# A spectral mix and a mixture of experts on one core: input pieces loaded as 112 rows plus one shared row, and four moves in the opening order

## The chip, the cores and the metric

The kernel runs on one core of a Trainium2 chip. The metric is device time in microseconds (us) of one execution. The kernel before takes 635.36 us (median of 3 runs, 635.27 to 635.87). The five engines are named here as the profile names them: PE (TensorE matmuls) with its weight loads PEld, DVE (VectorE), ACT (ScalarE), POOL (GpSimd), and SP, which only issues transfers.

## The reference

The kernel computes, for 2048 tokens `x` of width 448, a gated sum of two branches:

```python
g = sigmoid((x * gate_w).sum(-1, keepdims=True))
# branch a: real part of a 2-D Fourier transform by matrices
a_ = x @ dft_hid_re.T ; b_ = x @ dft_hid_im.T
a  = dft_seq_re @ a_ - dft_seq_im @ b_
# branch b: 8 experts, the two best per token
gates = softmax(x @ wg); top 2, renormalised -> cw
h = gelu(einsum("nd,edf->nef", x, w1)) ; y = einsum("nef,efd->ned", h, w2)
b = einsum("ne,ned->nd", cw, y)
out = g * a + (1 - g) * b
```

## The kernel before

**Stages.** From about 38 us to the end PE runs the experts, one unit (expert, 128 of its 1792 inner columns) after another: the first layer (line 752) and the second (line 803). The change lies wholly in the 38 us ahead of that, the opening, which has three jobs: the routing's logits and, from them, the list of the tokens of the first expert; the hidden-axis Fourier transform; and the sequence-axis transform. Both transforms use the matrices' mirror symmetry, so the tokens come as eight input pieces.

**Input pieces.** Piece (c, r), c = 0 to 3 and r = 0 or 1, is a slab of 128 partitions by 1024 numbers (4 KB per partition). A partition holds one hidden index; only the first 113 (`HH`) hold data, the rest zeros. SP issues the eight loads (line 102) in the order c, r, with the hidden matrix `wr` behind the fourth, then `spec` and the four sequence matrices `cw` (line 107). ACT's own queue issues one load, the logits' weights `wgr` (line 98). Each load signals one of eight semaphores in turn; a load that comes to a semaphore in use waits on SP for the load that had it.

**PE in the opening.** `logits(c)` (line 474) multiplies raw pieces with `wgr`; `flip(c)` (line 481) transposes the result, and after `flip(3)` the routing starts. `hidden(v)`, v = 0 to 7, called block v below, is the hidden transform of one folded half (line 512); ACT copies its result from PSUM to the tile `ab` (line 513). `even(m)`, m = 0 to 3 (line 453), multiplies the matrix `cw` m with blocks 0 to 3, in two halves of two products each; `odd(m, v)` (line 555) multiplies it with block v = 4 to 7, one product each. In the trace an f32 product is two matmul instructions with a weight load each, so an even(m) is 8 and an odd(m, v) is 2 of them, and a block 8. `turn_over(n)` (line 116) issues n matmuls on zeros.

**DVE in the opening.** Each piece is folded in three steps: `fold_near` (line 488), `fold_half` (lines 492 and 493) and `fold_quarter` (line 505). A fold_quarter(c, r) makes what block 2c + r multiplies. Between folds stands the routing, a generator whose steps `advance()` issues. Its steps here: the marks `mb` of each token's two experts (lines 243 to 256, DVE); the running counts `pt` (lines 259 to 262, PE, 18 matmuls); each token's position at the first expert, ending in the tile `ov` (lines 272 to 288, DVE); two short DVE lines for `dz` (291 and 292); the token list (line 296 on PE, line 300 as casts `tok` on DVE and ACT), from which POOL gathers rows (line 532); and on ACT the exponential `ex` with a load of the table for the next function behind it (lines 304 and 305).

**ACT behind it.** ACT then rounds the first two weight tiles (`upper`, line 205, four instructions, `hi` and `up` each) and only then copies blocks 6 and 7.

**What sets the order.** PE, DVE, ACT and SP run in the order in which the code issues; nothing is rescheduled. Each engine takes its instructions in that order, so one that waits holds all behind it.

Of the kernel before, what the change touches and what calls it, by code (L numbers as in the profile page):

```python
# [9 lines left out]
F32 = mybir.dt.float32  # L10
# [5 lines left out]
OP = mybir.AluOpType  # L16
AX = mybir.AxisListType

P = 128
# [28 lines left out]
NQT = QT // P  # L48
# [2 lines left out]
HD = D // 2 + 1  # L51
HE = HD + 1
HH = HE // 2
NL = 32
LOTS = (0, NF)
BANKS = (0, 1, 2, 4, 3)
# [15 lines left out]
def tile_kernel(ctx: ExitStack, tc: tile.TileContext, xt, xrows, xplain, wg, whid, cq, cw, cspec, edge, refs, wquad, whall, cgen, wcat, out):  # L72
    nc = tc.nc
    te, ve, se, gp, sp = nc.tensor, nc.vector, nc.scalar, nc.gpsimd, nc.sync
# [15 lines left out]
    hp = hid_stack.enter_context(tc.tile_pool(name="hid", bufs=2))  # L90
    XR = {}
# [4 lines left out]
    CW = [abp.tile([P, 2, NQT, P], F32, name="cw", bufs=NQT) for _ in range(NQT)]  # L96
    spec = keep.tile([P, 3 + NQT], F32, name="spec")
    se.dma_start(wgr, wg)
    for c in range(NQT):
        XR[c] = hp.tile([P, 2, 2, 2, 2, P], F32, name="xraw", bufs=NQT)  # L100
        for r in range(2):
            sp.dma_start(XR[c][:, r], xt[c + r * NQT])
        if c == 1:
            sp.dma_start(wr, whid)
    sp.dma_start(spec, cspec)
# [351 lines left out]
    def advance(n=1):  # L457
        for _ in range(n):
            next(route, None)
# [6 lines left out]
    def logits(c, *rs):  # L466
        if c not in LT:
            LT[c] = psy.tile([P, P], F32, name=f"y{1 + c % 2}")
        for s in range(4):
            cc, far = divmod(s, 2)  # L470
            for h in range(2):
                for r in rs:
                    j = 32 * (2 * h + r)
                    te.matmul(LT[c][j : j + 32], wgr[:, cc, far], XR[c][:, r, cc, far, 1 - h if far else h], start=s == 0, stop=s == 3, tile_position=(0, j))  # L474

    def evacuate(c):
        LT[c, 1] = hp.tile([P, P], F32, name="lgt")
# [5 lines left out]
    def fold_near(c, *rs):  # L483
        if c not in PQ:
            PQ[c] = hp.tile([P, 2, 2, 2, P], F32, name="pq")
            EO[c] = hp.tile([P, 2, 2, 2, P], F32, name="eo")
        for r in rs:
            ve.tensor_tensor(PQ[c][:, r], XR[c][:, r, :, 0], XR[c][:, r, :, 1], OP.add)

    def fold_half(c, r):  # L490
        raw, pq, eo = XR[c], PQ[c], EO[c]
        ve.tensor_tensor(eo[:, r, 0], pq[:, r, :, 0], pq[:, r, :, 1], OP.add)
        ve.tensor_tensor(eo[:, r, 1], pq[:, r, :, 0], pq[:, r, :, 1], OP.subtract)
        if c == 0:
            if r.start:
                ve.tensor_copy(xs, eo[:, 1, 0, :, 0:1].to_broadcast([P, 2, P]))
                for k in range(2):
                    ve.tensor_tensor(eo[:, k, 0, :, 0:1], raw[:, 0, :, 0, k, 0:1], raw[:, 0, :, 1, 1 - k, 0:1], OP.add)
                ve.memset(eo[:, 0, 1, :, 0:1], 0.0)

    def fold_quarter(c, *rs):
        if c not in FH:
            FH[c] = hp.tile([P, 2, 2, 2, P], F32, name="fr", bufs=NQT)
        for r in rs:
            ve.tensor_tensor(FH[c][:, r], EO[c][:, 0], EO[c][:, 1], OP.subtract if r else OP.add)

    def hidden(v):
        fr = FH[v // 2][:, v % 2]
        acc = ps.tile([P, 512], F32, name="acc")
        for u in range(2):  # L510
            for c in range(2):
                te.matmul(acc[:, 256 * u + HH * c : 256 * u + HH * (c + 1)], fr[:, u, c], wr[:, u, c], start=True, stop=True)  # L512
        se.activation(ab[:, v], halves(acc), AF.Copy)

    def special():
        acc = ps.tile([P, 512], F32, name="acc")
        for c in range(2):
            te.matmul(acc[:, HH * c : HH * (c + 1)], xs[:, c], wr[:, 0, c], start=True, stop=True)
        se.activation(mid[:, 1], acc[:, :HE], AF.Copy)


# [5 lines left out]
    def gather0(c, n):  # L527
        if c < FULL:
            XG[c] = r32(stream.tile([P, DX], F32R, name=("hi", "lo", "up", "dn")[c], bufs=3 if c < 2 else 4))
        else:  # L530
            XG[c] = xp.tile([P, NQ, P], F32, name="xg", bufs=2).rearrange("p q d -> p (q d)")
        gp.indirect_dma_start(out=XG[c][:n], out_offset=None, in_=xplain,
                              in_offset=bass.IndirectOffsetOnAxis(ap=rt["tok0"][:n, c : c + 1], axis=0))
# [8 lines left out]
    def even(m, between=None):  # L542
        acc = ps.tile([P, 512], F32, name="acc")
        for part in range(2):
            run_steps(acc[:, 256 * part : 256 * part + HE], [source(m, part, c) for c in (0, 1)])
            if between and part == 0:
                between()
        se.activation(fold[:, m, :, 0], halves(acc), AF.Copy)
# [44 lines left out]
    flip(3)  # L593
    fold_near(2, slice(0, 2))
    fold_half(2, slice(0, 2))
    fold_quarter(2, 0)
    se.activation(ch[:, :, 0:1], spec[:, 3:, None], AF.Copy)
    special()
    even(0)
    advance()  # L600
    even(1)
    advance()
    fold_quarter(2, 1)
    advance()
    for k in range(3):
        fetch(k)
    even(2)
    even(3)
    hidden(4)
    fold_near(3, 0)  # L610
    advance(2)
    for c, n in enumerate(tl0[:FULL]):
        gather0(c, n)
    hidden(5)
    advance()
    for v in (4, 5):
        for m in range(NQT):
            odd(m, v)
    upper(0)
    upper(1)  # L620
    fold_near(3, 1)
# [661 lines left out]
```

## Time and profile before

| | |
|---|---|
| median of 3 runs | 635.36 us (635.27 to 635.87) |
| profiled execution | 634.15 us |
| its span, first to last instruction | 632.2 us |
| PE busy in the span | 621.9 us (98%) |
| first matmul of the first expert (line 752) | 38.09 us |

A row of the timeline gives start, duration, engine, line, operation, out<-in and a count of merged instructions; in brackets stands the idle time of the engine ahead of it and what ended it. The ends of matmuls are modelled, so a merged row of PE overlaps the next one slightly; for pace the starts of weight loads (PEld) are the better clock.

### The profile page before, as it was taken

To read this page: it belongs to the slowest core of one execution; us is meant where nothing else is said; L and a number is where in the kernel's file an instruction comes from. 1 tells how busy PE (TensorE), PEld (TensorE's weight loads), DVE (VectorE), ACT (ScalarE), POOL (GpSimd) and SP (SyncE) were. 2 spreads that over 40 slices of the span, in tenths; PEclk is the share of its full clock that TensorE was granted. 3 is DMA by queue.
4 is the path that set the end of the run, shared out by engine and by line. 5 is a ranking of instruction groups with operands and counts; after the bars stand their busy time and mean duration, and the time that the engine had idled before them with its cause. 6 is when DMAs were issued, how large, how long until landed. Compare 5 with 4: busy or idle time off the path is not lost.

```text
span 632.2 us, 10955 instructions
## 1 busy us (share of the span) xinstructions
PE 621.9 (98%) x3595; PEld 557.2 (88%) x3595; DVE 503.4 (80%) x1258; ACT 289.4 (46%) x588; POOL 214.3 (34%) x194
## 2 busy tenths in 40 slices
PE   8999999999999999999999999999999999999994
PEld 5999999999998999989999788888888888888884
DVE  7889798679977999779896799988997778655560
ACT  2553233555565566564664434333343334434440
POOL 1210074645144353244450344333241442141123
PEclk9999999999999999999999999999999999999999
DMA  8546454597777777786776867879566737666755
GB/s 332 197 146 218 151 190 147 153 255 235 219 224 191 205 244 227 223 199 196 239 238 211 202 190 244 255 203 281 179 216 192 152 119 156 159 143 143 147 83 64
DMA packets 58751, 122.77 MB, mean 194 GB/s; under 512 B 8288, under 2 KB 31984, under 8 KB 58688
## 3 DMA queue, kind: packets, MB, share of 16 engines
q1 hardware_dynamic: 47376, 101.95, 49.7%
q0 software_dynamic: 11168, 20.00, 18.1%
q8 instruction: 30, 0.49, 0.3%
q14 instruction: 33, 0.27, 0.1%
q10 hardware_dynamic: 144, 0.07, 0.0%
HBM read 105.89 MB, written 16.08 MB: 193 GB/s over the span
## 4 chain that ended last, share of the span: by engine, by line
PE 93%; issue 3%; POOL 1%; DMA 1%; DVE 1%; POOLq 0%; ACT 0%; DVEq 0%; ACTq 0%
PE acc L752 45%; PE y L803 42%; PE y L820 1%; PE acc L512 1%; PE y L555 1%; POOL out L856 1%; PE y L474 1%; DMA wgr<-wg 1%; PE acc L453 0%; POOL out L1019 0%; PE acc L404 0%; PE y L116 0%; PE y L667 0%; PE acc L667 0%; POOLq L1050 0%
## 5 line engine op out<-in xcount | busy, mean ns | idle before, releaser
L752 PE MATMUL acc<-X,hi 128*128 128x288 f32 (+3 forms) x1050 | 215.6, 342 | 0.0
L637 POOL DMA_INDIRECT xg<-xrows,piece x115 | 126.3, 1098 | 210.5 <-DVE xq L646 127.8
L752 PEld LDWEIGHTS acc<-X,hi 128*128 128x128 f32 x1050 | 173.6, 188 | 19.4 <-issue 1.1
L803 PE MATMUL y<-dn,gh 128*128 128x448 f32 (+1 forms) x458 | 167.3, 365 | 0.0
L803 PE MATMUL y<-up,gh 128*128 128x448 f32 (+1 forms) x458 | 167.3, 365 | 0.0
L803 PE MATMUL y<-up,gl 128*128 128x448 f32 (+1 forms) x444 | 162.5, 366 | 0.0
L756 ACT ACTIVATE g<-acc 128x288 f32<-128x288 f32 (+3 forms) x126 | 61.9, 491 | 194.8 <-issue 109.2
L752 PE MATMUL acc<-X,lo 128*128 128x288 f32 (+3 forms) x672 | 134.6, 322 | 0.0
L752 PEld LDWEIGHTS acc<-X,lo 128*128 128x128 f32 x672 | 105.6, 188 | 10.2
L856 POOL DMA_INDIRECT out<-ys,tok x36 | 65.4, 1817 | 115.4 <-ACT ys L852 75.6
L770 DVE TENSOR_TENSOR gl<-g,gh 128x512 fp32r<-128x512 f32 (+1 forms) x111 | 76.5, 689 | 21.1 <-ACT gh L767 15.0
L803 PEld LDWEIGHTS y<-up,gh 128*128 128x128 f32 (+1 forms) x458 | 85.8, 187 | 7.5
L803 PEld LDWEIGHTS y<-dn,gh 128*128 128x128 f32 (+1 forms) x458 | 85.8, 187 | 7.5
L897 DVE CUSTOM_DVE_ANT_0 junk<-quads 128x512 f32<-128x512 f32 x128 | 87.9, 687 | 2.2
L803 PEld LDWEIGHTS y<-up,gl 128*128 128x128 f32 (+1 forms) x444 | 83.2, 187 | 7.1 <-DVE gl L770 0.2
L210 DVE TENSOR_TENSOR lo<-raw,hi 128x512 fp32r<-128x512 f32 x112 | 77.0, 687 | 1.6 <-ACT hi L205 0.6
L769 DVE CAST gh<-g 128x512 fp32r<-128x512 f32 (+2 forms) x69 | 30.2, 438 | 58.6 <-ACT g L756 58.3
L205 ACT ACTIVATE hi<-raw 128x512 fp32r<-128x512 f32 x112 | 69.4, 619 | 0.0
L210 DVE TENSOR_TENSOR dn<-row,up 128x448 fp32r<-128x448 f32 x112 | 69.1, 617 | 0.0
L205 ACT ACTIVATE up<-row 128x448 fp32r<-128x448 f32 x112 | 63.3, 565 | 0.0
L754 ACT ACTIVATE g<-acc 128x256 f32<-128x256 f32 x42 | 16.1, 383 | 49.2 <-PE acc L752 48.8
L1019 POOL DMA_DIRECT2D out<-ot x16 | 13.9, 866 | 60.2 <-ACT ot L1018 60.2
(265 smaller groups left out, 434.9 us busy)
## 6 DMA issues: line engine op xcount, KB each, us to landing
quads<-cq SPq DMA_DIRECT2D x64, 512.0 KB, 5.2
raw<-wcat SPq DMA_DIRECT2D x112, 256.0 KB, 3.0
row<-wcat SPq DMA_DIRECT2D x112, 224.0 KB, 3.5
out<-yt SPq DMA_DIRECT2D x21, 224.0 KB, 3.4
xraw<-xt SPq DMA_DIRECT2D x8, 512.0 KB, 7.0
out<-ot POOLq DMA_DIRECT2D x16, 224.0 KB, 3.9
cw<-cw SPq DMA_DIRECT2D x4, 512.0 KB, 9.5
xg<-xrows,piece POOLq DMA_INDIRECT x115, 3.6
```

Source lines behind the costliest of these rows:

```text
L205: se.activation(hi[:, : raw.shape[-1]], raw, AF.Copy)
L210: ve.tensor_tensor(lo[:, :n], raw, r32(hi[:, :n]), OP.subtract)
L637: st = gp.indirect_dma_start(out=xg[:, q], out_offset=None, in_=xrows, in_offset=bass.IndirectOffsetOnAxis(ap=rt["piece"][:, e, g : g + 1] ...
L752: te.matmul(acc[:, :m], a, b, start=s == 0, stop=s == len(steps) - 1)
L754: se.activation(g[:, cs], acc[:, n : 2 * n], AF.Copy)
L756: se.activation(g[:, cs], g[:, cs] if both else acc[:, :n], AF.Gelu_apprx_tanh)
L769: ve.tensor_copy(gh[:, :top], g[:, :top])
L770: ve.tensor_tensor(gl[:, :main], g[:, :main], r32(gh[:, :main]), OP.subtract)
L803: te.matmul(Y[c][:m, :D], a, b, start=f == 0 and s == 0, stop=f == NF - 1 and s == len(steps) - 1)
L856: st = gp.indirect_dma_start(out=out, out_offset=bass.IndirectOffsetOnAxis(ap=rt["tok"][:n, e, c : c + 1], axis=0), in_=ys[:n], in_offset= ...
L897: ve.tensor_tensor_reduce(out=junk[:, :512], in0=row(a[0])[:, a[1] * 512 : a[1] * 512 + 512], in1=row(b[0])[:, b[1] * 512 : b[1] * 512 + 5 ...
L1019: st = gp.dma_start(out[i * P : (i + 1) * P, :], ot[:, :D], accum_op=OP.add)
```

## The change

The code does four things.

1. The eight input loads carry 112 partitions instead of 128 (`EVEN = 112`), into one tile `xraw`. Partition 112 of all eight pieces comes in one load of 8 rows of 4 KB, issued on ACT's queue behind `wgr`. The folds and products on the pieces read 113 partitions.
2. fold_quarter(2, 0) moves from ahead of the marks to behind them; fold_quarter(2, 1) moves from behind the counts to behind block 4, which puts it behind the positions on DVE; fold_near(3, 0) moves behind the token list.
3. The first half of even(2), two products, moves ahead of the counts.
4. Block 5 moves behind the four odd(m, 4).

```diff
+EVEN = 112
...
     se.dma_start(wgr, wg)
+    xraw = hp.tile([P, 2, NQT, 2, 2, 2, P], F32, name="xraw", bufs=1)
+    se.dma_start(xraw[EVEN:HH].rearrange("p r c a f h t -> p (r c) (a f h t)"), xt[:, EVEN:HH].rearrange("k p a f h t -> p k (a f h t)"))
     for c in range(NQT):
-        XR[c] = hp.tile([P, 2, 2, 2, 2, P], F32, name="xraw", bufs=NQT)
+        XR[c] = xraw[:HH, :, c]
         for r in range(2):
-            sp.dma_start(XR[c][:, r], xt[c + r * NQT])
+            sp.dma_start(xraw[:EVEN, r, c], xt[c + r * NQT, :EVEN])
...
     fold_half(2, slice(0, 2))
-    fold_quarter(2, 0)
     se.activation(ch[:, :, 0:1], spec[:, 3:, None], AF.Copy)
     special()
     even(0)
     advance()
     even(1)
-    advance()
-    fold_quarter(2, 1)
+    fold_quarter(2, 0)
+    even(2, advance)
     advance()
     for k in range(3):
         fetch(k)
-    even(2)
     even(3)
     hidden(4)
+    fold_quarter(2, 1)
+    advance(2)
     fold_near(3, 0)
-    advance(2)
     for c, n in enumerate(tl0[:FULL]):
         gather0(c, n)
+    for m in range(NQT):
+        odd(m, 4)
     hidden(5)
     advance()
-    for v in (4, 5):
-        for m in range(NQT):
-            odd(m, v)
+    for m in range(NQT):
+        odd(m, 5)
     upper(0)
     upper(1)
     fold_near(3, 1)
```

On PE, behind the 16 matmuls of the token list, before: `acc_487` is block 5 and the next two groups of four are odd(m, 4) and odd(m, 5); `acc_527` and `acc_533` are blocks 6 and 7.

```order
L512 MATMUL acc_487<-wr_81,fr_323 128x113 x4
L555 MATMUL y0_497<-ab_82,cw_84 128x226
L555 MATMUL y1_499<-ab_82,cw_85 128x226
L555 MATMUL y2_501<-ab_82,cw_86 128x226
L555 MATMUL y4_503<-ab_82,cw_87 128x226
L555 MATMUL y0_497<-ab_82,cw_84 128x226
L555 MATMUL y1_499<-ab_82,cw_85 128x226
L555 MATMUL y2_501<-ab_82,cw_86 128x226
L555 MATMUL y4_503<-ab_82,cw_87 128x226
L512 MATMUL acc_527<-wr_81,fr_524 128x113 x4
L512 MATMUL acc_533<-wr_81,fr_524 128x113 x4
```

The same place on PE in the changed kernel, where `acc_493` is block 5.

```order
L558 MATMUL y0_485<-ab_82,cw_84 128x226
L558 MATMUL y1_487<-ab_82,cw_85 128x226
L558 MATMUL y2_489<-ab_82,cw_86 128x226
L558 MATMUL y4_491<-ab_82,cw_87 128x226
L515 MATMUL acc_493<-wr_81,fr_360 128x113 x4
L558 MATMUL y0_485<-ab_82,cw_84 128x226
L558 MATMUL y1_487<-ab_82,cw_85 128x226
L558 MATMUL y2_489<-ab_82,cw_86 128x226
L558 MATMUL y4_491<-ab_82,cw_87 128x226
L515 MATMUL acc_525<-wr_81,fr_522 128x113 x4
L515 MATMUL acc_531<-wr_81,fr_522 128x113 x4
```

Block 5 now stands directly ahead of the four products that multiply it, where four others stood between.

On ACT, from the copy of block 4 on, in the changed kernel (`acc_493` is block 5, `acc_525` and `acc_531` blocks 6 and 7):

```order
L516 ACTIVATE ab_82<-acc_442 128x452
L303 CAST tok0_469<-acc_452 32x5 x2
L516 ACTIVATE ab_82<-acc_493 128x452
L307 ACTIVATE ex_499<-dz_449 128x32
L308 ACT_TABLE_LOAD
L308 ACTIVATE table_501<-rev_130 128x1
L208 ACTIVATE hi_507<-raw_415 128x512
L208 ACTIVATE up_509<-row_416 128x448
L208 ACTIVATE hi_513<-raw_428 128x512
L208 ACTIVATE up_515<-row_429 128x448
L516 ACTIVATE ab_82<-acc_525 128x452
L516 ACTIVATE ab_82<-acc_531 128x452
```

Nothing moved on ACT here: the order is that of before, with three lines added to each line number.

On DVE, the start of the folds in the changed kernel, with the semaphores that each instruction waits for:

```order
L491 TENSOR_TENSOR pq<-xraw 113x512 [waits DMAHW2_49,DMAHW1_49]
L495 TENSOR_TENSOR eo<-pq 113x256 [waits DVE_49]
L496 TENSOR_TENSOR eo<-pq 113x256
L491 TENSOR_TENSOR pq<-xraw 113x512 [waits DMAHW3_49]
L495 TENSOR_TENSOR eo<-pq 113x256 [waits DVE_49]
```

The first fold waits for two loads now, its own piece (DMAHW2) and the shared row (DMAHW1); the later ones wait for their piece alone. On PE the first logits product waits for these two and `wgr`.

## Rows read from the trace of the kernel before

**Rows 1.** The page: busy time, share of the span and instructions of PE.

```profile
PE 621.9 (98%) x3595; PEld 557.2 (88%) x3595; DVE 503.4 (80%) x1258; ACT 289.4 (46%) x588; POOL 214.3 (34%) x194
```

**Rows 2.** All waits of PE in the whole span: engine, what waited, for what, us in total, times, longest.

```profile
PE y L116 <- DVE warm L111: 1.4, 1, 1.4
PE y L259 <- DVE mb L256: 0.5, 1, 0.5
PE y L474 <- DMA wgr<-wg: 0.3, 1, 0.3
```

**Rows 3.** The chain of work that ended last, in order of time, from 0 to 46 us: start, us, what.

```profile
0.91 4.44 DMA wgr<-wg
...
17.13 0.30 DVE mx L243
...
20.76 0.30 DVE mb L256
...
32.36 1.61 PE y L555 x8
```

**Rows 4.** Timeline of PE's weight loads, 8 to 17 us.

```profile
8.68 0.14 PEld L474 LDWEIGHTS y<-xraw,wgr 128*32 128x32 f32 x2 [0.42 <-issue]
...
10.04 1.86 PEld L512 LDWEIGHTS acc<-wr,fr 128*128 128x128 f32 x16 [0.20 <-DVE fr L505]
12.01 0.99 PEld L474 LDWEIGHTS y<-xraw,wgr 128*32 128x32 f32 x32
13.20 0.20 PEld L481 LDWEIGHTS y<-ident,lgt 128*128 128x128 f32 x2 [0.20 <-issue]
...
14.44 0.14 PEld L474 LDWEIGHTS y<-xraw,wgr 128*32 128x32 f32 x2
...
15.77 0.14 PEld L481 LDWEIGHTS y<-ident,lgt 128*128 128x128 f32 x1 [0.20 <-issue]
```

**Rows 5.** Transfers of the opening: the issue of `wgr` on ACT's queue (timeline); the input pieces, KB each and median us from issue to landing; the least, median and greatest of these; the stretch 5 to 10 us with busy time of PE, PEld, DVE, ACT and POOL, granted clock, share of the 16 transfer engines and GB/s.

```profile
0.91 0.41 ACTq L98 DMA_DIRECT2D wgr<-wg  x1
...
xraw<-xt SPq DMA_DIRECT2D x8, 512.0 KB, 7.0
...
DMA to landing us min/median/max: 4.2/7.0/9.0
...
5.00:10.00 5.00, 4.69 (x70) 2.87 (x69) 4.74 (x13) 0.28 (x1) 0.00 (x0) 1.00 1.03 416
```

**Rows 6.** Timeline of DVE: the first fold, fold_quarter(2, 0), the start of the marks, fold_quarter(2, 1), the last of the positions.

```profile
5.16 0.69 DVE L488 TENSOR_TENSOR pq<-xraw 128x512 f32<-128x512 f32 x1 [3.00 <-DMA xraw<-xt]
...
16.07 0.69 DVE L505 TENSOR_TENSOR fr<-eo 128x512 f32<-128x512 f32 x1
17.13 0.29 DVE L243 TENSOR_REDUCE mx<-y 128x16 f32<-128x128 f32 x1 [0.36 <-PE y L481]
...
20.97 0.68 DVE L505 TENSOR_TENSOR fr<-eo 128x512 f32<-128x512 f32 x1
...
25.07 0.49 DVE L288 TENSOR_TENSOR ov<-og,tokid 128x320 f16<-128x320 f32 x1
```

**Rows 7.** Timeline of PE and its weight loads, 17 to 34 us: even(0) and even(1), the counts, even(2) and even(3), block 4, the token list, block 5, the odd products, blocks 6 and 7, odd(m, 6).

```profile
17.26 2.97 PEld L453 LDWEIGHTS acc<-ab,cw 128*128 128x128 f32 x16
...
20.24 0.10 PEld L259 LDWEIGHTS <-tri 128*128 128x128 bf16 x1
...
21.10 0.22 PE L259 MATMUL y<-mb,tri 128*128 128x136 bf16 x1 [0.51 <-DVE mb L256]
...
21.75 2.97 PEld L453 LDWEIGHTS acc<-ab,cw 128*128 128x128 f32 x16
...
24.73 1.05 PEld L512 LDWEIGHTS acc<-wr,fr 128*128 128x128 f32 x8
...
25.89 0.46 PEld L296 LDWEIGHTS <-oh 128*32 128x32 f16 x16
...
26.37 0.97 PEld L512 LDWEIGHTS acc<-wr,fr 128*128 128x128 f32 x8
...
27.26 2.98 PEld L555 LDWEIGHTS y<-ab,cw 128*128 128x128 f32 x16
...
30.24 1.94 PEld L512 LDWEIGHTS acc<-wr,fr 128*128 128x128 f32 x16
...
32.20 1.78 PE L555 MATMUL y<-ab,cw 128*128 128x226 f32 x8
```

**Rows 8.** Timeline of ACT from the copy of block 5 to that of block 7.

```profile
27.56 0.55 ACT L513 ACTIVATE ab<-acc 128x452 f32<-128x452 f32 x1 [0.35 <-PE acc L512]
28.00 0.22 ACT L304 ACTIVATE ex<-dz 128x32 f32<-128x32 f32 x1
28.23 1.28 ACT L305 ACT_TABLE_LOAD   x1
...
29.63 0.61 ACT L205 ACTIVATE hi<-raw 128x512 fp32r<-128x512 f32 x1
...
31.61 0.52 ACT L513 ACTIVATE ab<-acc 128x452 f32<-128x452 f32 x1
32.40 0.55 ACT L513 ACTIVATE ab<-acc 128x452 f32<-128x452 f32 x1 [0.27 <-PE acc L512]
```

More of the change, by code (lines that the diff above doesn't have):

```diff
@@ L473, in logits @@
                     j = 32 * (2 * h + r)
-                    te.matmul(LT[c][j : j + 32], wgr[:, cc, far], XR[c][:, r, cc, far, 1 - h if far else h], start=s == 0, stop=s == 3, tile_position=(0, j))
+                    te.matmul(LT[c][j : j + 32], wgr[:HH, cc, far], XR[c][:, r, cc, far, 1 - h if far else h], start=s == 0, stop=s == 3, tile_position=(0, j))
     def evacuate(c):
@@ L487, in fold_near @@
         for r in rs:
-            ve.tensor_tensor(PQ[c][:, r], XR[c][:, r, :, 0], XR[c][:, r, :, 1], OP.add)
+            ve.tensor_tensor(PQ[c][:HH, r], XR[c][:, r, :, 0], XR[c][:, r, :, 1], OP.add)
     def fold_half(c, r):
-        raw, pq, eo = XR[c], PQ[c], EO[c]
+        raw, pq, eo = XR[c], PQ[c][:HH], EO[c][:HH]
         ve.tensor_tensor(eo[:, r, 0], pq[:, r, :, 0], pq[:, r, :, 1], OP.add)
@@ L495, in fold_half @@
             if r.start:
-                ve.tensor_copy(xs, eo[:, 1, 0, :, 0:1].to_broadcast([P, 2, P]))
+                ve.tensor_copy(xs[:HH], eo[:, 1, 0, :, 0:1].to_broadcast([HH, 2, P]))
                 for k in range(2):
@@ L504, in fold_quarter @@
         for r in rs:
-            ve.tensor_tensor(FH[c][:, r], EO[c][:, 0], EO[c][:, 1], OP.subtract if r else OP.add)
+            ve.tensor_tensor(FH[c][:HH, r], EO[c][:HH, 0], EO[c][:HH, 1], OP.subtract if r else OP.add)
     def hidden(v):
-        fr = FH[v // 2][:, v % 2]
+        fr = FH[v // 2][:HH, v % 2]
         acc = ps.tile([P, 512], F32, name="acc")
@@ L511, in hidden @@
             for c in range(2):
-                te.matmul(acc[:, 256 * u + HH * c : 256 * u + HH * (c + 1)], fr[:, u, c], wr[:, u, c], start=True, stop=True)
+                te.matmul(acc[:, 256 * u + HH * c : 256 * u + HH * (c + 1)], fr[:, u, c], wr[:HH, u, c], start=True, stop=True)
         se.activation(ab[:, v], halves(acc), AF.Copy)
@@ L517, in special @@
         for c in range(2):
-            te.matmul(acc[:, HH * c : HH * (c + 1)], xs[:, c], wr[:, 0, c], start=True, stop=True)
+            te.matmul(acc[:, HH * c : HH * (c + 1)], xs[:HH, c], wr[:HH, 0, c], start=True, stop=True)
         se.activation(mid[:, 1], acc[:, :HE], AF.Copy)
```

## The prediction

> **What bounds the kernel now.** I read the page first, then the waits of PE, then the chain, then the opening engine by engine. PE is busy 98% of the span [rows 1], and in the whole span it is shown waiting only three times, all before 21.1 us [rows 2]. So from 38 us on the kernel is a row of matmuls in fixed order, and the change, which stops short of them, is worth what it moves the first expert's start. In the opening the chain [rows 3] goes over the landing of `wgr`, PE's logits, DVE's marks (17.13 to 21.06) and then PE again, without a hole, to the experts. I take four things from there: when the first product can start, what the pieces cost on the way, what the 0.51 us ahead of the counts is worth, and what moving block 5 does to ACT.
>
> **Part 1: the start.** The first fold began at 5.16, on its piece [rows 6]; the first logits product on `wgr`, 4.44 us after its issue at 0.91 [rows 3], at 5.35. Now both also need the shared row, which ACT issues when it has issued `wgr`, at 0.91 + 0.41 = 1.32 at the earliest [rows 5]. No row shows a load of one partition. Bounds: not before `wgr`, which stands ahead of it in the same queue, so a cost of 0; and the slowest input piece took 9.0 us to land [rows 5], which gives 10.3, a cost of 5.0. The nearest row is `wgr`, same queue and same moment: with its 4.44 us the row lands at 5.76, 0.4 us later than before. I take +0.4. DVE's folds start 0.6 us later (5.76 for 5.16); that was covered by nothing before, but fold_quarter(2, 0) no longer stands ahead of the marks, so DVE has until flip(3): folds ended at 16.76, the marks started at 17.13, and taking 0.69 away leaves 16.07 + 0.6 = 16.7, still ahead of it [rows 6].
>
> **Part 2: smaller pieces.** From 5 to 10 us the transfers ran at 416 GB/s [rows 5]; at that rate a piece of 512 KB took 1.26 us; at 448 KB it is 1.10, and the eighth piece comes 8 x 0.16 = 1.25 us sooner, less 0.08 for the 32 KB of the shared row. What PE gains is only what it waited. A logits group of 32 products with nothing missing took 13.20 - 12.01 = 1.19 us; the ones that missed a piece took 10.04 - 8.68 = 1.36 and 15.77 - 14.44 = 1.33 [rows 4]. That is 0.17 + 0.14 = 0.31 us, and with the start 0.4 later it is gone even if the pieces come no faster, but for a tenth or so. I take -0.3. The sum of parts 1 and 2 is +0.1 at flip(3), bounds -0.3 and +4.7.
>
> **Part 3: the moved folds and the two even products.** Moving fold_quarter(2, 0) gives nothing by itself: the marks started on PE's flip, 0.36 us after DVE was free [rows 6]. It now lies where fold_quarter(2, 1) lay (20.97), in which DVE waits for the counts anyway. fold_quarter(2, 1) is behind the positions, fold_near(3, 0) behind the token list: the same DVE work in another order, and its results are read later (below). PE waited 0.51 us for `mb` [rows 7]. Two even products are four of the 16 loads in 2.98 us (17.26 to 20.24), 0.75 us: PE is through with them at 20.99, and the last needs one more pace of 0.19, so the counts start at about 21.2 for 21.10. The wait is filled and the counts are 0.1 late, and with them DVE's positions: 25.56 becomes 25.66. Counted by the modelled matmul ends the delay would be 0.3; bounds 0 and 0.3. PE then has 0.75 us less ahead of the token list: before, it came to the list at 25.89, when the positions had been done for 0.3 us. Now it comes at about 25.89 + 0.1 - 0.75 = 25.24 and waits for the positions until 25.72. Of 0.51 us, 0.17 is left; the rest has become a wait at the token list, for DVE.
>
> **Part 4: block 5 later.** This is the term that decides. Before: list 25.89, block 5 at 26.37, its copy on ACT at 27.56 [rows 7, 8]. Now: list 25.72, the four odd(m, 4) at 25.72 + 0.48 = 26.20; they are half of 2.98 us, 1.49, so block 5 starts at 27.69 and its copy, 1.19 us behind that as before, at 28.88: 1.32 us later (1.49 - 0.17). Two things wait for this copy. On PE, odd(m, 5) stands right behind block 5: it starts at 28.88 + 0.55 + 0.04 = 29.47, where PE was free at about 28.8, a wait of 0.7 that did not exist, because the odd(m, 4) covered it. On ACT, the exponential, the table load of 1.28 us and the four roundings stand behind it in a row without a hole, and behind these the copy of block 6: from 27.56 to 31.61, 4.05 us, ending at 32.13 [rows 8]. ACT can't take block 6 earlier; its order has not changed. So block 6 is in `ab` at 28.88 + 4.05 + 0.52 = 33.45. PE had started odd(m, 6) at 32.20 [rows 7], with 0.07 us to spare; it now starts at 33.49. PE's own way there, 29.47 + 1.49 for odd(m, 5) and 1.94 for blocks 6 and 7, is done at 32.9, so the 0.7 us is contained in the later wait, not added to it. That is +1.29 at odd(m, 6). Bounds: if only PE's wait counted, 32.9 - 32.2 = +0.7; if the counts are 0.3 late, +1.5. DVE's last folds come later by the one fold_near that went behind the list, 0.7 us (0.69 in rows 6), and blocks 6 and 7, which read them, also start 0.7 later (29.47 + 1.49 = 30.96 for 30.24). POOL's gathers start with the token list, which moves by 0.2 us, and are read 1.3 us later. So nothing but ACT decides there, and behind it stands the same PE work as before, in which no wait can give the time back [rows 2].
>
> **The sum.** +0.1 + 1.3 = +1.4 us. On the profiled execution of 634.15 us (span 632.2 and 1.95 outside it) that gives 635.6; on the median of 635.36, which lies 1.2 above it, 636.8. What a measurement of this kernel can tell from no change is about 0.2%, 1.27 us.
>
> **Rivals.** *The shared row comes late.* Eight rows of 4 KB go into one partition, and the first product and the first fold wait for all. Against it: it is 32 KB, 0.08 us at the rate of rows 5. For it: all eight share one destination, and pieces have landed up to 9.0 us after issue. I work it for a landing between `wgr`'s 4.44 us and the median piece's 7.0: 1.32 + 5.2 = 6.5, so PE starts 1.15 us late, gets 0.3 back, and DVE's folds, 1.35 late, hold block 2 for another 0.1. That gives +0.95 + 1.3 = +2.2, 637.6. Each further us of delay costs one. The Trainium skill has a rule for this in SBUF — State Buffer, section Door 1: the DMA port swizzle: bandwidth goes by how many of 16 ports the partitions reach, and four neighbouring partitions, one port, were measured at 27.6 GB/s. By that rule an estimate for 32 KB through one port is 1.2 us rather than 0.08; no row of the trace has a transfer into a single partition, so nothing here says whether it holds. With it the row lands at 6.9 and the sum would be 638.0, inside the span of this rival.
>
> *Block 5's delay is covered.* The price of part 4 falls away if PE has 1.3 us of other work ahead of odd(m, 6), that is, if block 6's copy is not the last to come. Then what is left is 0.17 at the list and 0.3 on the pieces, less 0.4 for the start or nothing: -0.5 to -0.1; I put it at 635.0, which is not slower. It decides from the point where the copy of block 6 may end 1.3 us after 32.13 and PE still finds it done. Against it stands the 0.07 us of spare in the trace and an ACT without a hole from 27.56 to 32.13 [rows 7, 8].
>
> *The start comes earlier.* If the smaller pieces let `wgr` and the shared row land with the first piece, PE starts at 5.16 for 5.39, and with the 0.3 of part 2 the opening gains 0.5 ahead of flip(3): -0.5 + 1.3 = +0.8, 636.1. For it: `wgr`'s 64 KB share the engines with pieces that are an eighth smaller. Against it: behind the first piece stands the second, so the engines are as full as before.
>
> *The loads aren't split as meant*, and the first product waits for all eight pieces, since they are one tile now: the last is first read at 14.44 [rows 4], some 9 us of loss. The waits in the program's order name one piece and the shared row, so I give it 1 in 100.
>
> **How the numbers follow.** Forecast 0.60 at 636.8 (its own range 636.2 to 637.3); the late row 0.21 at 637.6 and up to 638.3; covered 0.09 at 635.0; early start 0.09 at 636.1; one tile 0.01. The range 635.7 to 638.1 leaves out most of the covered case and the far end of the late row, less than 2 in 10. The border of slower by 0.2% is 636.63: about two thirds of the forecast and all of the late row lie above it, 0.60; faster by 0.2%, below 634.1, would need more than all that the opening waits, 0.04; the rest, 0.36, is within.
>
> **What the profile of the changed kernel would show.** Part 1: the first logits product and the first fold released by `xraw` at 5.7 to 5.8, not by `wgr`. Part 2: logits groups of 1.19 us throughout. Part 3: no wait ahead of the counts, and a wait of about 0.4 ahead of the token list, for DVE's `ov`. Part 4: a wait on ACT of 0.6 to 0.7 between block 5 and odd(m, 5), another of about 0.5 ahead of odd(m, 6), the copy of block 6 ending 1.3 us later than before counted from flip(3), and the first matmul of the experts at about 39.5 for 38.09. I am wrong if odd(m, 6) starts less than half a us later than before, counted from flip(3); if the first product starts after 6 the late row is true.

## The result and the profile after

The changed kernel takes 640.40 us (median of 6 runs, 639.88 to 641.21), the kernel before in runs taken beside it 635.36 (6 runs, 634.97 to 635.87). The ratio is 1.0078, with a 95% interval of 1.0067 to 1.0089: 5.0 us slower. The sign was forecast, the size was not; 640.4 lies 2.3 us above the range.

| profiled execution | before | after |
|---|---|---|
| time | 634.15 us | 640.1 us |
| span | 632.2 us | 638.1 us |
| first logits product (PE) | 5.39 | 7.90 |
| start of the marks, `mx` (DVE) | 17.13 | 20.51 |
| first matmul of the experts (PE) | 38.09 | 42.84 |
| from `mx` to the experts | 20.96 | 22.33 |

The last row is the new order: +1.37 us, forecast +1.3. The loads are in the row of the marks: +3.38 us, forecast +0.1. Line numbers of after are 3 higher than those of before.

All waits of PE in the whole span of after (as [rows 2]):

```profile
PE y L477 <- DMA xraw<-xt: 3.1, 1, 3.1
PE y L119 <- DVE warm L114: 1.4, 1, 1.4
PE y L806 <- ACT hi L208: 1.1, 1, 1.1
PE y L558 <- ACT ab L516: 0.6, 1, 0.6
PE y L558 <- issue: 0.5, 1, 0.5
PE acc L299 <- DVE ov L291: 0.4, 1, 0.4
```

`warm` is there in both kernels. The wait of 0.5 for `mb` ahead of the counts is gone, and the 0.4 at the token list, the 0.6 ahead of odd(m, 5) and the 0.5 ahead of odd(m, 6) are those that the prediction named. New and large is the 3.1 for the input ahead of the first product. The 1.1 at line 806 lies far behind the opening, at 133 us (below).

The stretch 5 to 10 us of after: busy time of PE, PEld, DVE, ACT and POOL, granted clock, share of the transfer engines and GB/s (as the last of [rows 5]):

```profile
5.00:10.00 5.00, 2.10 (x17) 1.63 (x18) 2.07 (x5) 0.00 (x0) 0.00 (x0) 0.76 1.01 254
```

The transfer engines are as full as before (share 1.01 for 1.03) and move 254 GB/s instead of 416. At 254 GB/s a piece of 448 KB takes 1.81 us, and 1.69 at the 272 that loads of 112 rows reach alone (rates, below); one of 512 KB took 1.26. The pieces have become smaller and slower.

Timeline of DVE and of ACT's queue in after: the first fold, the start of the marks; the issues of `wgr` and of the shared row.

```profile
7.86 0.69 DVE L491 TENSOR_TENSOR pq<-xraw 113x512 f32<-113x512 f32 x1 [5.71 <-DMA xraw<-xt]
...
20.51 0.29 DVE L246 TENSOR_REDUCE mx<-y 128x16 f32<-128x128 f32 x1 [1.77 <-PE y L484]
```

```profile
0.92 0.42 ACTq L99 DMA_DIRECT2D wgr<-wg  x1
1.37 1.24 ACTq L101 DMA_DIRECT2D xraw<-xt  x1
```

The issue of the shared row alone takes ACT 1.24 us, three times `wgr`'s.

Timeline of PE in after, from the first product on:

```profile
7.90 1.92 PE L477 MATMUL y<-xraw,wgr 113*32 113x128 f32 x16 [3.06 <-DMA xraw<-xt]
9.75 1.41 PE L119 MATMUL y<-warm 128*128 128x512 bf16 x3
11.10 1.07 PE L477 MATMUL y<-xraw,wgr 113*32 113x128 f32 x16
...
12.63 1.08 PE L477 MATMUL y<-xraw,wgr 113*32 113x128 f32 x32
...
15.61 1.08 PE L477 MATMUL y<-xraw,wgr 113*32 113x128 f32 x32
16.62 0.44 PE L484 MATMUL y<-ident,lgt 128*128 128x128 f32 x2
...
17.87 1.35 PE L477 MATMUL y<-xraw,wgr 113*32 113x128 f32 x32
19.15 0.33 PE L484 MATMUL y<-ident,lgt 128*128 128x128 f32 x1
...
29.09 0.56 PE L299 MATMUL acc<-ov,oh 128*32 128x20 f16 x16 [0.42 <-DVE ov L291]
...
32.90 1.79 PE L558 MATMUL y<-ab,cw 128*128 128x226 f32 x8 [0.64 <-ACT ab L516]
...
36.92 1.80 PE L558 MATMUL y<-ab,cw 128*128 128x226 f32 x8 [0.46 <-issue]
...
42.84 1.10 PE L755 MATMUL acc<-X,hi 128*128 128x256 f32 x7
```

Timeline of PE and of its weight loads in before, the second logits group and the last one:

```profile
7.15 1.07 PE L474 MATMUL y<-xraw,wgr 128*32 128x128 f32 x16
...
14.76 0.81 PEld L474 LDWEIGHTS y<-xraw,wgr 128*32 128x32 f32 x30 [0.18 <-DMA xraw<-xt]
```

The way of PE to +3.38 at the marks is in these rows. PE starts 2.51 us later (7.90 for 5.39). It had stood idle for 3.06 us, and the first 16 products and the turn_over behind them take 3.20 us to the next group (7.90 to 11.10) where before they took 1.76 (5.39 to 7.15): +1.44. The granted clock was 0.50 from 8 to 10 us, the lower of its levels, 1.2 GHz. Then the logits groups of 32 products wait less for pieces (1.01, 1.01 and 1.28 us from start to start for 1.36, 1.19 and 1.32), and 0.57 comes back. 2.51 + 1.44 - 0.57 = 3.38.

What ended last on this way is the eighth piece. A group with nothing missing takes 1.01 us; the last one, 1.28 from 17.87 on, still waited for it (two weight loads at 17.87, the other 30 from 18.15 on), as the last one of before had (two at 14.44 [rows 4], 30 from 14.76 on). The trace's marks of landing have the eighth piece at 18.11 us, before at 14.72: +3.39, all of the delay at the marks. PE's late and slow start is contained in this wait, not added to it; by itself, as these rows let one estimate, it would have brought the marks 3.1 us late, 0.27 less.

### The profile page after: what moved, and what is told of

Its sections match the earlier page's. It is cut to its first block, busy times and chain, and to the rows that moved or that the text cites. A ratio compares the mean times of both kernels' runs of the same rounds, so it can differ in the third digit from the quotient of the medians.

```text
span 638.1 us, 10958 instructions
## 1 busy us (share of the span) xinstructions
PE 622.9 (98%) x3595; PEld 557.5 (87%) x3595; DVE 502.7 (79%) x1258; ACT 287.5 (45%) x588; POOL 215.0 (34%) x194
## 5 line engine op out<-in xcount | busy, mean ns | idle before, releaser
L759 ACT ACTIVATE g<-g 128x256 f32<-128x256 f32 x42 | 17.6, 418 | 45.1 <-DVE g L758 37.8
```

The source lines that it names most:

```text
L759: se.activation(g[:, cs], g[:, cs] if both else acc[:, :n], AF.Gelu_apprx_tanh)
```

## The experiments

Times at the experts' first matmul are of the one profiled execution of each kernel, before: 38.09. Ratios are to the kernel before, run on the same chip.

### Which half: order_only and loads_only

`order_only` has the loads of before and the code order of after; `loads_only` the loads of after and the order of before.

```diff
 order_only, against after
-            sp.dma_start(xraw[:EVEN, r, c], xt[c + r * NQT, :EVEN])
+            sp.dma_start(XR[c][:, r], xt[c + r * NQT])
...
 loads_only, against after
-    for m in range(NQT):
-        odd(m, 4)
     hidden(5)
     advance()
-    for m in range(NQT):
-        odd(m, 5)
+    for v in (4, 5):
+        for m in range(NQT):
+            odd(m, v)
...
```

> The kernel before with its own loads of 128 rows and all the moves of the new order (parts 3 and 4 of the change alone). If block 5's delay on ACT's path costs what the trace of after suggests: marks at 17.1 as before, a wait of about 0.4 us ahead of the token list for ov, 0.6 to 0.7 ahead of odd(m, 5) for ACT's copy, about 0.5 ahead of odd(m, 6), first matmul of the experts at 39.4 to 39.5 for 38.09, and a time 1.3 us above the kernel before (636.7). If the delay was a follow-on of the late and slow start instead: no such waits, 38.1, 635.3.

Measured: 636.44 us for 635.26, ratio 1.0022 (1.0014 to 1.0031), +1.2 us. Timeline of PE in order_only:

```profile
25.69 0.56 PE L296 MATMUL acc<-ov,oh 128*32 128x20 f16 x16 [0.43 <-DVE ov L288]
...
29.50 1.79 PE L555 MATMUL y<-ab,cw 128*128 128x226 f32 x8 [0.64 <-ACT ab L513]
...
33.52 1.79 PE L555 MATMUL y<-ab,cw 128*128 128x226 f32 x8 [0.46 <-ACT ab L513]
...
39.43 1.10 PE L752 MATMUL acc<-X,hi 128*128 128x256 f32 x7
```

Three waits at their places, +1.34 at the experts. Here the wait ahead of odd(m, 6) is put down to ACT's copy by name. Parts 3 and 4 hold without the loads.

> The changed kernel's loads (112 rows and the shared row) with the order of the kernel before. If the two halves of the change add up: the marks 3.4 us later (20.5 for 17.13), nothing more behind them, a time 3.4 to 3.7 us above the kernel before (638.8 to 639.1). If the old order can take some of the late start back (fold_quarter(2, 0) stands ahead of the marks again, the counts wait again): 3.9 to 4.2. If the loads cost nothing by themselves and only their meeting with the new order did: below 636.

Measured: 639.62 us for 635.26, ratio 1.0069 (1.0054 to 1.0085), +4.4 us. The first product starts at 7.73, the experts at 42.01, +3.92. The time is above each of the ranges; the 3.92 lie in the second (3.9 to 4.2), but not for its reason: the marks are already 3.9 us late here for 3.4 in after, because both groups of 16 products are slow. The last group waits for no piece here (the eighth landed at 17.67). Timeline of PE in loads_only:

```profile
7.73 1.92 PE L477 MATMUL y<-xraw,wgr 113*32 113x128 f32 x16 [2.33 <-DMA xraw<-xt]
9.58 1.46 PE L119 MATMUL y<-warm 128*128 128x512 bf16 x3
10.97 1.92 PE L477 MATMUL y<-xraw,wgr 113*32 113x128 f32 x16
```

Both groups are slow, 1.92 us for 16 products. The view of this trace gives a granted clock of 1.00 for 5 to 15 us, but that isn't a reading: the trace's first entry of the clock, a rise, is at 13.00 us, and the view counts the time ahead of it as full. The pace shows the level: the three turn_overs between the groups take 1.39 us to the next start (9.58 to 10.97), as in after at a clock of 0.50 (1.35, from 9.75 to 11.10), where before took 0.76 at 1.00 (6.39 to 7.15). So PE ran at the lower level here until about 13 us; in the trace of before the first entry, also a rise, is at 4.63.

### Which load: no_row and row_128

`no_row` drops the shared row and reads 112 rows, so hidden index 112 is left out of the logits and the transform; `row_128` keeps the 128-row pieces and adds the shared row's load, with something on PE and DVE that waits for it.

```diff
 no_row, against loads_only
-    se.dma_start(xraw[EVEN:HH].rearrange("p r c a f h t -> p (r c) (a f h t)"), xt[:, EVEN:HH].rearrange("k p a f h t -> p k (a f h t)"))
-        XR[c] = xraw[:HH, :, c]
+        XR[c] = xraw[:EVEN, :, c]
...
 row_128, against before (both: one tile for ab and cw, loaded over later)
+    se.dma_start(both[:1].rearrange("p (k n) -> p k n", k=2 * NQT), xt[:, 112:113].rearrange("k p a f h t -> p k (a f h t)"))
...
+    ve.tensor_copy(tiny[:1], both[:1, :1])
+    te.matmul(idle[:32, :64], both[:1, :32], both[:1, 32:96], start=True, stop=True)
```

> loads_only without the load of the shared row: folds and products read 112 rows, so hidden index 112 is left out of logits and transform. If 112 rows are slow by themselves: the input still moves at 250 to 290 GB/s from 5 to 15 us, a piece takes 1.6 to 1.75 us; the first product starts at 5.4 to 6.0, but the later logits groups then wait for their pieces, and the marks still come 2 us or more late (19 or later), 637.4 or more. If the shared row is what slowed the transfers: 400 GB/s or more, the first product at 5.3 to 5.5, the marks at 17.1 or a little before, 635.0 to 635.4.

Measured: 638.07 us, ratio 1.0052 (1.0038 to 1.0067), +2.8 us. The stretch 5 to 10 us, and PE:

```profile
5.00:10.00 5.00, 4.51 (x39) 2.54 (x39) 4.20 (x12) 0.28 (x1) 0.00 (x0) 1.00 1.04 289
```

```profile
5.88 1.77 PE L476 MATMUL y<-xraw,wgr 112*32 112x128 f32 x16 [0.49 <-DMA wgr<-wg]
...
14.36 1.07 PE L476 MATMUL y<-xraw,wgr 112*32 112x128 f32 x30 [0.46 <-DMA xraw<-xt]
...
17.62 1.07 PE L476 MATMUL y<-xraw,wgr 112*32 112x128 f32 x30 [0.59 <-DMA xraw<-xt]
```

Without the shared row the first product starts at 5.88, but the pieces still come at 289 GB/s: the sixth at 14.36, the eighth at 17.62, 1.63 us each, and PE waits for them. The eighth landed at 17.57, 2.85 later than before, and the experts start at 40.95, +2.86. The 112 rows are slow by themselves.

> The kernel before (128 rows, old order) with the load of the shared row added on ACT's queue behind wgr, into a tile of its own at partition 0; one small product on PE and one copy on DVE wait for it ahead of the first logits product and the first fold. If the row is late because of itself (eight rows of 4 KB into one partition, an issue of 1.24 us): transfers of 410 GB/s beside it, and it still lands at 7.0 to 7.7; the marks 1.5 to 3 us later (18.6 to 20), the time 1.5 to 3 us above the kernel before. If it was late only because the 112-row pieces were slow: it lands at 5.8 to 6.3, the marks at 17.5 to 18, the time 0.3 to 0.9 above.

Measured: the pieces run at 384 GB/s from 5 to 10 us, and the row still comes at 7.4. Timeline of PE in row_128:

```profile
7.46 0.42 PE L573 MATMUL y<-both 1*32 1x64 f32 x2 [2.07 <-DMA both<-xt]
7.81 1.92 PE L478 MATMUL y<-xraw,wgr 128*32 128x128 f32 x16
```

So the row is late by itself: it lets PE start 2.07 us later than `wgr` did before (7.46 for 5.39). Of that, 0.47 is that ACT issues it behind `wgr` (1.38 for 0.91) and 0.8 the longer issue (1.23 for 0.41), if a landing is counted from the end of its issue; no row gives a cause for the rest. The marks start at 20.11, just above the 18.6 to 20 expected, and the experts at 41.16, +3.07, of which 0.35 is the added product. The total, 643.63 us (ratio 1.0145, 1.0130 to 1.0161), is 6 us more than that and isn't read as the row's price: from 400 to 550 us this kernel's PE issued 230 or 231 matmuls in 50 us where before issued 234 or 235, and why the merged tile does that was not followed up.

Either fault alone costs about 3 us at the experts, both together 3.9 (loads_only): behind a late start the slow pieces have time to land.

### Is it the idle PE: warm_more

```diff
 against loads_only
-WARM = 9
+WARM = 19
```

> loads_only with ten more matmuls on zeros (19 for 9) ahead of the first logits product, so that PE does not stand idle for 2.3 us before it. If the slow pace behind that idle time (16 products in 1.92 us, three turn_overs in 1.46) is a cost by itself: the first groups take 1.07 us and the turn_overs 0.8, and flip(3) ends about 1.0 earlier than in loads_only, at 19.7 to 19.9 for 20.73; not more, because no_row shows that the eighth piece lands at 17.6, so a wait of 0.3 to 0.9 for xraw appears in the later logits groups; first matmul of the experts at 41.0 to 41.2 for 42.01, a time about 1 us below loads_only. If the pieces alone set the end: no change, 42.0.

Measured: 639.79 us, ratio 1.0060 (1.0041 to 1.0080), runs from 637.58 to 641.79; no gain that can be told from loads_only. PE and the stretch 5 to 10 us in warm_more:

```profile
8.02 1.07 PE L477 MATMUL y<-xraw,wgr 113*32 113x128 f32 x16
...
16.28 1.07 PE L477 MATMUL y<-xraw,wgr 113*32 113x128 f32 x30 [0.99 <-DMA xraw<-xt]
...
19.98 1.08 PE L477 MATMUL y<-xraw,wgr 113*32 113x128 f32 x30 [1.05 <-DMA xraw<-xt]
```

```profile
5.00:10.00 5.00, 4.86 (x34) 2.26 (x34) 1.98 (x4) 0.00 (x0) 0.00 (x0) 1.00 1.02 241
```

The first half is as expected: PE is kept busy, the clock rises at 5.93, and the products take 1.07 at once. The gain is lost to the pieces, which came at 241 GB/s in this execution (loads_only 270 with the same loads); the eighth landed at 19.94, and the experts started at 43.32. In this execution the slow pace was gone and nothing was won: a PE that is ready earlier waits for the pieces.

That idle time keeps the clock down is not shown by this alone. In the three executions in which PE stood idle for 2.1 to 3.1 us (after, loads_only, row_128) the pace of the first products was low until 10.8 to 13.0 us; in the seven others of this opening the clock had risen by 7.4. But in no_block5 it rose only at 7.24 without any idle time, and the first 16 products took 1.92 us there as well.

### Why 112 rows are slow: rates, rates2, rates3, rates4

Each is the kernel before with sets of loads of the same data ahead of its own.

```diff
 rates (rates2 alike with 124, 127, 113)
+    for n in (128, 112, 120, 96):
+        for c, r in flat if n in (128, 120) else flat[::-1]:
+            sp.dma_start(XR[c][:n, r], xt[c + r * NQT, :n])
...
 rates4 (rates3 without the last line, and with set 4)
+    for step, (a, b, d) in enumerate(((32, 32, 64), (32, 64, 96), (64, 64, 112))):
+        for c in cs:
+            rows(sp, c, 0, a)
+            rows(se, c, b, d)
+        rows(sp, cs[-1], 0, P)
```

> The kernel before with 41 loads of the same data put ahead of its own, so only its first stretch is read: 8 loads of 128 rows of 4 KB, 8 of 112, 8 of 120, 8 of 96, 4 of 64 neighbouring rows of 8 KB, 4 of every other row (64 of 128) of 8 KB, and one of a single row of 8 KB. Each set begins when the last load of the set ahead has landed. If a row count that doesn't lay whole port groups on whole engines is what slows the pieces: 128 rows at about 410 GB/s, 120 rows (8 for each of 15 engines) at about 385, 112 rows at 250 to 290, 96 no faster than 290, 64 neighbouring rows near 200, every other row faster than these. If rows are alike and the shared row or the reading kernel was the cause: 112, 120 and 96 rows all at 400 or more.

Measured, the inside of each set of rates, in the order 128, 112, 120, 96, 64 neighbouring rows, every other row; the last two columns are the share of the transfer engines and GB/s:

```profile
5.00:11.00 6.00, 0.39 (x1) 0.00 (x0) 0.00 (x0) 0.00 (x0) 0.00 (x0) 0.85 1.03 419
17.00:27.00 10.00, 0.00 (x0) 0.00 (x0) 0.00 (x0) 0.00 (x0) 0.00 (x0) 0.50 1.03 272
32.00:44.00 12.00, 0.00 (x0) 0.00 (x0) 0.00 (x0) 0.00 (x0) 0.00 (x0) 0.50 0.96 239
50.00:58.00 8.00, 0.00 (x0) 0.00 (x0) 0.00 (x0) 0.00 (x0) 0.00 (x0) 0.50 1.03 249
65.00:72.00 7.00, 0.00 (x0) 0.00 (x0) 0.00 (x0) 0.00 (x0) 0.00 (x0) 0.50 1.04 209
77.00:81.00 4.00, 0.00 (x0) 0.00 (x0) 0.00 (x0) 0.00 (x0) 0.00 (x0) 0.50 0.99 340
```

Only 128 rows move at over 400 GB/s. With 112 rows all engines are busy (1.03) and two thirds of the rate is left, with no other work on the core. 120 rows at 239 is a miss of mine: fifteen engines with eight rows each were to give 385.

> The kernel before with 32 loads put ahead of its own, only its first stretch is read: 8 loads of 124 rows of 4 KB, 8 of 127, 8 of 113, then 4 of the upper 64 rows of 8 KB and 4 of 128 rows of 8 KB; each set begins when the last load of the set ahead has landed. If only a load of all 128 rows lies right on engines and ports: 124 and 127 rows at 250 to 300 GB/s or less, 113 (a prime number of rows) lower still, 64 upper rows near 205 as the 64 lower ones, 128 rows at 410. If slowness grows with the rows that are missing: 124 and 127 near 400, 113 near 280.

Measured: 124 rows at 105 GB/s, then 127 and 113 rows:

```profile
12.00:40.00 28.00, 0.00 (x0) 0.00 (x0) 0.00 (x0) 0.00 (x0) 0.00 (x0) 1.00 0.26 105
100.00:300.00 200.00, 0.00 (x0) 0.00 (x0) 0.00 (x0) 0.00 (x0) 0.00 (x0) 1.00 0.06 26
```

The shares are 4/16 and 1/16 of full: 124 rows used four engines, 127 and 113 one, at 26 GB/s each. The upper 64 rows ran at 207, as the lower. So 113 rows in one load, the obvious other way to write this change, would have moved at a tenth of the rate of 112. The Trainium skill says how many engines a load gets (DMA: Bandwidth & Descriptors, section Why a DMA increments its semaphore by 16 and not by 1): the largest number up to 16 that divides the rows. The shares 0.26, 0.06 and, for 120 rows, 0.96 agree.

> The kernel before with four sets of loads put ahead of its own, only its first stretch is read. Set 1: 4 pairs, rows 0 to 31 (8 KB each) on SP's queue beside rows 32 to 63 on ACT's. Set 2: the same with rows 64 to 95 on ACT's queue in place of rows 32 to 63: as many rows, bytes and loads, other partitions. Set 3: 4 pairs, rows 0 to 63 on SP's queue beside rows 64 to 111 on ACT's. Set 4: 4 loads of 128 rows of 2 x 3.5 KB. If it matters which partitions are written at one time (ports): set 1 near the 205 GB/s of 64 neighbouring rows, set 2 well above it (300 to 400); set 3 between 280 and 400. If only the split of rows over engines matters: sets 1 and 2 alike. Set 4 about 400 either way, an eighth less time a load than 128 rows of 8 KB: bytes taken off the rows are saved, rows taken off are not.

Measured: inconclusive for sets 1 to 3. ACT's queue ran ahead of SP's, the sets mixed, and the mixture moved at 205 to 223 GB/s from 4 to 22 us and at 141 to 186 from there to 32. Set 4, rows shortened to 3.5 KB but all 128 of them, ran at 391 GB/s.

> The first three sets of rates3 again, now kept apart: after each set a load of 128 rows of 8 KB, which begins when the set has landed and ends before the next begins. Set 1, rows 0 to 31 on SP's queue beside rows 32 to 63 on ACT's; set 2, rows 0 to 31 beside rows 64 to 95; set 3, rows 0 to 63 beside rows 64 to 111. If it matters which partitions are written at one time: set 1 at about 205 GB/s, set 2 at 300 to 400, set 3 at 280 or more. If only the split of rows over engines matters: sets 1 and 2 alike.

Measured, set 1, a load of 128 rows between, set 2, set 3:

```profile
5.00:11.00 6.00, 0.39 (x1) 0.00 (x0) 0.00 (x0) 0.00 (x0) 0.00 (x0) 1.00 1.04 207
15.00:17.00 2.00, 0.00 (x0) 0.00 (x0) 0.00 (x0) 0.00 (x0) 0.00 (x0) 1.00 1.02 414
20.00:26.00 6.00, 0.00 (x0) 0.00 (x0) 0.00 (x0) 0.00 (x0) 0.00 (x0) 1.00 1.03 267
38.00:49.00 11.00, 0.00 (x0) 0.00 (x0) 0.00 (x0) 0.00 (x0) 0.00 (x0) 1.00 1.04 243
```

Sets 1 and 2 have the same rows, bytes, loads and queues; moving half of them from partitions 32 to 63 to 64 to 95 gives 267 for 207. So it matters which partitions are written at one time, but 267 is below the 300 to 400 expected, so that is not the whole of it. Set 3, which has the rows 0 to 111 of the pieces, split over two queues, ran at 243 where at least 280 was expected. The Trainium skill's SBUF — State Buffer, section Door 1: the DMA port swizzle, puts partitions 0 to 63 on 8 of 16 ports and gives 196 GB/s for them; 209 and 207 here are near it. By the Trainium skill's table there, 112 rows put eight rows on 12 of the ports, as 128 rows do on all 16, so an estimate by this table alone is that no time could be saved; that a piece takes 1.69 us instead of 1.26 it doesn't say. With 128 rows each engine has a port of its own, says the Trainium skill (DMA: Bandwidth & Descriptors, section The descriptor swizzle). That with 112 rows engines meet at ports would fit; no run here shows which engine writes where, and why 112 rows are slow stays open.

### The new order taken apart: no_block5, act_late, fill

```diff
 no_block5, against order_only: block 5 back in its place
+    hidden(5)
+    advance()
     for m in range(NQT):
         odd(m, 4)
...
 act_late, against order_only
-    upper(0)
-    upper(1)
     fold_near(3, 1)
...
     hidden(7)
+    upper(0)
+    upper(1)
 fill, against before
+    even(2, counts)
     even(3)
     hidden(4)
...
+    hidden(5, tokens)
```

In `fill`, `counts` and `tokens` issue the steps of the routing between the two halves of even(2) and of block 5.

> order_only (loads of 128 rows, new order) with block 5 put back ahead of the odd(m, 4); the moved folds and the two even products stay. If block 5's place is the whole cost of the new order: no wait ahead of the counts, about 0.4 us ahead of the token list for ov, none ahead of odd(m, 5) and odd(m, 6), the experts' first matmul at 37.9 (0.17 earlier than 38.09), a time of 635.0 to 635.2, the same as the kernel before. If the moved folds or the split even(2) cost something too: 38.4 or later, 635.7 or more.

Measured: 634.26 us for 634.36, ratio 1.0001 (0.9992 to 1.0010); the experts start at 38.06. The whole cost of the new order is block 5's place; the rest of it is worth nothing that can be measured. Of the 0.17 expected at the experts nothing came: block 5 starts 0.69 us behind the token list for 0.49 before, at 26.36, right behind its fold, fold_quarter(2, 1), which in this order stands behind the positions and ends at 26.21.

The same trace shows what a start that is only a little late costs. PE in no_block5, the second logits group:

```profile
7.94 1.07 PE L474 MATMUL y<-xraw,wgr 128*32 128x128 f32 x16
```

It starts 0.79 us later than before (7.15), and the marks start at 17.08 for 17.13; in order_only it starts at 7.58 and the marks at 17.11. Up to 0.8 us went into the waits for pieces.

> order_only with the four roundings (upper) moved behind the copies of blocks 6 and 7 on ACT. If ACT's queue behind block 5's copy is what holds odd(m, 6): the wait of 0.46 us ahead of odd(m, 6) goes, it starts at 32.9 to 33.0 for 33.52, the wait of 0.64 ahead of odd(m, 5) stays, the experts' first matmul at 38.8 to 38.9 for 39.43, a time 0.5 to 0.6 us below order_only (635.8 to 635.9). If something else held it (PE's or DVE's own work): no change, 636.4. If the later roundings are missed at the experts: a wait of about 1 us at line 752 and no gain.

Measured: 636.20 us for 634.36, ratio 1.0032 (1.0021 to 1.0042). PE in act_late:

```profile
32.95 1.71 PE L555 MATMUL y<-ab,cw 128*128 128x226 f32 x8
...
37.50 0.66 PE L667 MATMUL y<-ident,up 128*128 128x128 f32 x4 [0.43 <-DVE fold L558]
...
41.98 0.85 PE L752 MATMUL acc<-X,hi 128*128 128x320 f32 x4 [0.53 <-DVE X L676]
```

odd(m, 6) starts at 32.95 without a wait: ACT's queue was what held it. But nothing is gained. DVE's own half of the rounding (line 210) waits 3.55 us for the later roundings and pushes DVE's copies behind it, PE waits 0.43 for one of them, and the experts start at 39.43 as in order_only. Within the first expert PE then waits 0.53 for the tile `X` from DVE; 1.34 + 0.53 is near the 1.84 between the medians.

> The kernel before with its loads and folds, two even(2) products ahead of the counts as in the change, and in place of block 5's move the first half of block 5 (two products, 0.49 us) ahead of the token list. If PE's wait of 0.51 us ahead of the counts only goes when other work also fills the wait that it turns into at the token list: no wait at either place, list at 25.8, block 5's copy at 27.0 for 27.56, odd(m, 6) at 31.6 for 32.20, the experts' first matmul at 37.5 to 37.6, a time 0.5 to 0.6 us below the kernel before (634.7). If something behind (rounded weights, gathered rows) is due at 38.1 anyway: a new wait there, 635.3.

Measured: 633.77 us for 634.36, ratio 0.9993 (0.9984 to 1.0002). PE in fill:

```profile
25.82 0.56 PE L296 MATMUL acc<-ov,oh 128*32 128x20 f16 x16
...
36.72 0.63 PE L674 MATMUL y<-ident,dn 128*128 128x128 f32 x4 [0.26 <-DMA dn<-xplain,tok]
```

Both waits are filled, and odd(m, 6) starts at 31.82 for 32.20. Then PE waits for the gathered rows `dn`, and the experts start at 38.19. The gathers start with the token list, which hangs on DVE's positions; POOL began the first at 27.74 (before 27.77), and the third took 1.42 us for 1.00 here. It is the fastest of the kernels, but no difference from before is shown.

## Why the prediction was wrong

**Part 1, the start: mis-sized.** "The nearest row is `wgr`, same queue and same moment: with its 4.44 us the row lands at 5.76." What waits for it began at 7.86 in after, at 7.7 in loads_only and at 7.44 in row_128, beside pieces at 384 GB/s. `wgr` is 128 rows into 128 partitions; the row goes into one partition, and its issue takes 1.24 us for 0.42. The upper bound of 5.0 held it. The rival of the late row was right in its sign, the first product started after 6, but its 637.6 to 638.3 were 2 us short: it took the pieces to come at the full rate. The estimate worked out from the Trainium skill (SBUF — State Buffer, section Door 1: the DMA port swizzle), 6.9, was nearer than mine and still early.

**Part 2, smaller pieces: the step that failed.** "At that rate a piece of 512 KB took 1.26 us; at 448 KB it is 1.10." The 416 GB/s were a rate of loads of 128 rows; I took it as a rate of the transfer engines. 112 rows ran at 241 to 289 GB/s in the kernels and at 272 alone, so the eighth piece landed 3.39 us later (18.11 in after for 14.72), not 1.25 us sooner, and the marks came 3.38 late behind it. No bound of part 2 had a loss in it; this alone costs 2.9 us at the experts (no_row).

**The path to the marks: misread.** The prediction followed the chain of [rows 3], over PE, and gave each us of delay ahead of the first product a price of one, less 0.3 that PE had waited for pieces. It read 1.19 us as the time of a logits group with nothing missing; such a group takes 1.01 (after, 15.61 to 16.62), so the three groups of before had waited 0.8 and not 0.3, and up to 0.8 us of delay cost nothing (no_block5). Beyond that either of two things can end last: the eighth piece, as in after, or PE, whose slow first products, 1.44 us in after, had no term in the prediction, as in loads_only. That the two lie within 0.3 us of each other in after is a coincidence.

**Part 3: right.** No wait ahead of the counts; 0.42 at the token list where 0.4 was forecast.

**Part 4: right.** odd(m, 6) is 16.41 us behind `mx` for 15.07 before: +1.34, forecast +1.29. The waits are 0.64 (0.6 to 0.7) and 0.46 (about 0.5). The copy of block 6 starts 36.35 - 32.30 = 4.05 us behind that of block 5, as in [rows 8]; no_block5 and act_late show the place of block 5 and ACT's queue as its cause.

**The sum.** +3.38 + 1.37 = +4.75 us at the experts; the medians differ by 5.0. The profiled executions differ by 5.95, since one more wait, of 1.1, stands at line 806 in that of after. The profiled one of before, 634.15, lies below all six of its timed runs (634.97 to 635.87), so these may have had that wait too; no trace shows it. A wait of 0.4 to 1.1 us at this place is in the traces of order_only, no_row, loads_only and warm_more too, one of 0.3 in rates and rates2, none in the others. It goes back to DVE's copy `wgt` near 100 us, which began 2.6 us after the products that it reads had ended (at 96.03, right behind them, before). What held DVE there was not found.

## What to carry to other kernels

The rate of a load is the rate of its shape: a transfer share of 1.0 at 416 GB/s belongs to 128 partitions, and taking rows off can cost more time than the bytes are worth, while taking bytes off each row nearly keeps the rate (391 GB/s at 128 x 7 KB). Before splitting a remainder off into a load of its own, look at what waits for it first and at how long its issue takes. Before pricing a late start, look at what the last piece of work in the stretch waits for: here a start 0.8 us late cost nothing, and a late last piece cost all. An engine's in-order queue makes a delay of one instruction a delay of everything behind it; follow the moved step through each queue it stands in, which here gave the new order's cost to a tenth of a us.

## What was not expected of the hardware

- Loads of 4 KB rows, GB/s by number of rows: 128: 419, 120: 239, 112: 272, 96: 249, 124: 105, 127 and 113: 26.
- The same eight loads of 112 rows ran at 241 GB/s in one execution (warm_more) and 270 in another (loads_only) from 5 to 10 us; the runs of loads_only spread over 2.8 us and those of warm_more over 4.2, those of order_only over 1.2.
- The issue of a load of eight 4 KB rows into one partition took 1.24 us on ACT, that of 128 rows of 512 B 0.42.
- PE's first 16 products took 1.92 us for 1.07 where the clock was 0.50 (after) or its first rise in the trace came later: loads_only (13.00), row_128 (10.81) and no_block5 (7.24), the last without any wait ahead of them.
